# Two low pieces of a weight matrix are made only after the first division by the softmax sums

## The chip, the cores and the metric

The kernel runs on one core of one Trainium2 chip. The metric is the time of one execution in microseconds (us), measured on the device; a kernel's time is the median of several runs. Beside the times there is one execution recorded by the hardware profiler, whose span runs from its first to its last instruction. The core has TensorE (PE, matrix products), VectorE (DVE), ScalarE (ACT), GpSimd (POOL) and SyncE (SP, which here only issues DMA transfers). Each engine runs its instructions in the order written; they wait for each other by semaphores.

## The reference, cut to what matters

The input x has 2048 rows of 640 numbers. Attention with a sliding window of 256 keys (32 heads of 20 numbers) and an MLP with a squared relu follow each other, twice, with the same weights both times:

```python
x = x + A(layernorm(x), wqkv, wo)
x = x + B(layernorm(x), w1, b1, w2, b2)
x = x + A(layernorm(x), wqkv, wo)
x = x + B(layernorm(x), w1, b1, w2, b2)

# A: 32 heads, causal, window of 256
q, k, v = split(x @ wqkv)
p = softmax(where(mask, q @ k.T * 20 ** -0.5, -1e9))
return (p @ v) @ wo
# B: 640 -> 1536 -> 640
h = relu(x @ w1 + b1)
return (h * h) @ w2 + b2
```

The order of the work that the change touches belongs to the start of the first layer: while the first rows go through attention, the weights are still being read and converted.

## The kernel before, in words

**Units and stages.** The rows are cut into 8 groups of 256, and the two layers make 16 units (u = 0 to 15). A unit goes through queries and keys (`stage_qk`), values (`stage_v`), scores, exponentials and products with the values in 8 "quads" of four heads (`max_quad`, `exp_quad`, `pv_quad`), the division by the softmax sums (`load_o`), the output projection with the residual sum and the second layernorm (`stage_o`, `stage_y`), and the MLP (`stage_f`). Units overlap: while the quads of unit u run, TensorE fills its gaps with the dense matrix products of the units beside it (`together`; for the first unit `flow`).

**Halves of 16 bits.** Each float32 matrix is split into a high half, a float16 copy, and a low half, the float16 residual. A product is then three matmuls: high times high, high times low, low times high (`mm3`, L327). For a weight the split is `convert` (L257): ScalarE writes the high half (L259), then VectorE writes the residual (L260).

**The second MLP matrix.** `load_w2` reads w2 in 12 pieces c = 0 to 11, each of 128 x 640 numbers, into five staging places: two in value buffers of later units (pieces 0 and 1) and three in the key buffer of unit 2 (the others, each place several times). The loads are issued on ScalarE's queue (L312). A piece that uses a place again is loaded after the residual of the piece that had it: piece 6 after piece 3, piece 7 after piece 4, then 9 after 6 and 10 after 7. After pieces 7 to 11 the key buffer is filled with a constant (`set_row`, L96, on VectorE), and then the keys of unit 2 are loaded into it (`spread` in `leave`, L548, on SP). After pieces 0 and 1 VectorE fills the sum columns in the two value buffers (L85, L86), which the values of unit 2 need. `stage_f` of unit 0 needs the pieces of w2 one by one.

**The division.** `pv_quad` leaves the products with the values and the sums in device memory. `load_o` reads them back (L871, L872) and divides in four quarters of 64 columns: the reciprocal of the sums (`ratio`, L904, VectorE), the product (`times`, L907, VectorE), the high half (`high`, L911, ScalarE), the low half (`low`, L914, VectorE). The list `js` holds the four low-half jobs. `stage_o` of a unit waits for the first two quarters, makes 30 matmuls with `wo` for the first 128 rows, adds the result to the residual stream (L939), starts a layernorm on it (L353 to L366), and does the same for the other 128 rows. `stage_y` turns the normalised rows over on TensorE (L391), with copies by L377 (ScalarE) and L378 (VectorE).

**The scores.** They are computed twice: once for the row maxima (matmuls L653 into the banks `bb`, maxima L633 on VectorE, eight for each quad), once for the exponentials (matmuls L757 or L765 into the same banks, L779 on ScalarE, masks L794 and L798 on GpSimd). A quad's products with the values are L828, copied out by L840 on ScalarE.

**The planner.** The order of instructions on each engine is fixed when the program is built. The work is posted as jobs with an engine, an estimated cost, the jobs that they depend on and a priority (0 is first, 2 last). `pump` places jobs at the planner's own clock: of the jobs that can start within the next 250 ns, it takes the first by priority; another job of that engine goes ahead of it only if it ends before the first can start. Residuals of w2 have priority 2, the division of unit 0 has priority 1 (its first two high halves 0), the maxima and the layernorms of `stage_o` 1, the additions L939 0. A job may also hold a list `gates` of marks that become done when it does. Three such marks hold loads of weights back already (`gate`, `gate0`, `gate2`):

```python
def put(self):
    t = self.start() + self.cost
    self.fn()
    clk[self.eng] = t
    self.end = t + TAIL[self.eng]
    ...
    for g in self.gates:
        g.end = self.end
```

Of the kernel before, what the change touches and what calls it, by code (L numbers as in the profile page):

```python
# [14 lines left out]
ALU = mybir.AluOpType  # L15
# [3 lines left out]
S = 2048  # L19
D = 640  # L20
# [25 lines left out]
def kernel(ctx: ExitStack, tc: tile.TileContext, x, wqkv, wo, w1, b1, w2, b2, out):  # L46
# [37 lines left out]
    def set_sums(i):  # L84
        nc.vector.memset(vts[i][0][:, :, DH:DH + 1], 1.0 / OS)  # L85
        nc.vector.memset(vts[i][1][:, H * (DH + 1):], 0.0)  # L86
# [8 lines left out]
    def set_row(i, k):  # L95
        nc.vector.memset(krow[i][:, 512 * k:512 * (k + 1)], PAIR)  # L96
# [36 lines left out]
    def post(eng, cost, fn, *deps, wait=0.0, prio=1, **kw):  # L133

        j = Job(eng, cost, fn, [d for d in deps if d is not None], now[0] + wait, prio, **kw)
        k = len(pend)
        while k and pend[k - 1].prio > prio:
            k -= 1
        pend.insert(k, j)
        return j  # L140

    def bulk(fn, size, *deps, **kw):

        return post("A", 400.0, fn, *deps, prio=2, size=size, idle=True, land=WLAND, **kw)

    def dma(fn, size, *deps, n=1, cost=450.0, prio=1, **kw):

        return post("S", n * cost, fn, *deps, prio=prio, size=size, **kw)
# [98 lines left out]
    w2_s = sb.tile([P, 2, FC, D], F16, name="w2_s")  # L247
# [6 lines left out]
    hraw = sb.tile([P, 2 * FC * T // 2], F32, name="stg", tag="hh", bufs=1)  # L254
    gate, gate0, gate2 = [Job("S", 0.0, None, [], 0.0, 0) for i in range(3)]

    def convert(st, hi, low, n, load, *deps, prio=2):  # L257

        a = post("A", 20 + 0.9 * n, lambda: nc.scalar.activation(hi, st, AF.Copy, scale=WS), load, *deps, prio=prio)  # L259
        return post("D", 30 + 1.04 * n, lambda: nc.vector.scalar_tensor_tensor(low, st, WS, hi, op0=ALU.mult,  # L260
                                                                               op1=ALU.subtract), a, prio=prio)

    wqj, woj, w1j, w2j = {}, {}, {}, {}

    def load_wq():
        at = 0
        for lo, n in [(j * D + c, min(2 * P, D - c)) for c in (0, 2 * P, 4 * P) for j in range(2)] + [
                (2 * D + c, min(2 * P, D - c)) for c in (0, 2 * P, 4 * P)]:
            raw, o = (w1raw, at) if at + KC * n <= FC * D else (krow[2], at - FC * D)
            at += KC * n  # L270
            st = raw[:, o:o + KC * n].rearrange("p (c n) -> p c n", c=KC)
            load = dma(lambda st=st, lo=lo, n=n:
                       nc.sync.dma_start(st, wqkv[:, lo:lo + n].rearrange("(c p) n -> p c n", p=P)),
                       P * KC * n * 4, prio=0, land=WLAND)
            for z in range(0, n, P):
                c = slice(lo + z, lo + z + P)
                wqj[(lo + z) // P] = convert(st[:, :, z:z + P], wq_s[:, 0, :, c], wq_s[:, 1, :, c], KC * P, load,
                                             prio=1)
# [3 lines left out]
    def load_wo():  # L282

        v = wo.rearrange("(h c d) n -> d h c n", c=KC, d=4)
        raw = w2raw[:, (FC - KC) * D:].rearrange("p (c n) -> p c n", n=D)
        loads = []
        for d in range(4):
            loads.append(bulk(lambda d=d: nc.scalar.dma_start(raw[d * H:(d + 1) * H], v[d]), H * KC * D * 4, gate0))
        for c in range(KC):
            woj[c] = convert(raw[:, c], wo_s[:, 0, c], wo_s[:, 1, c], D, loads[-1], *loads[:-1])  # L290
        rowset[1] = [post("D", 460, lambda k=k: set_row(1, k), prio=2) for k in range(4)]
# [11 lines left out]
                                 load, *first)  # L303

    sums = []

    def load_w2():
        used_by = {}
        for c, place in enumerate((3, 4, 0, 1, 2, 0, 1, 2, 0, 1, 2, 0)):
            first = [w1j[f] for f in (c // 4 * 2, c // 4 * 2 + 1, 6 + c // 4 * 2, 7 + c // 4 * 2)]  # L310
            st = vts[1 + place][1][:, :D] if place > 2 else krow[2][:, D * place:D * (place + 1)]
            load = bulk(lambda st=st, c=c: nc.scalar.dma_start(st, w2[c * P:(c + 1) * P, :]), P * D * 4,  # L312
                        *([w2j[used_by[place]]] if place in used_by else [gate] if place > 2 else [gate, gate2]))
            w2j[c] = convert(st, w2_s[:, 0, c], w2_s[:, 1, c], D, load, *first)
            used_by[place] = c
        sums.extend(post("D", 130, lambda i=i: set_sums(4 + i), w2j[used_by[3 + i]], prio=2) for i in range(2))

# [85 lines left out]
    def xsrc(l, b):  # L403
        return x_rows[b * P:(b + 1) * P, :] if l == 0 else xs[b]
# [452 lines left out]
    def load_o(u, late=False, free_=()):  # L857

        l, g = divmod(u, NG)
        if late:  # L860
            val = sb.tile([P, KC, T], F32, name="ov", tag="qt", bufs=2)
            od = sb.tile([P, KC, 2, T], F16, name="od", tag="yT", bufs=1)
        else:
            raw = sb.tile([P, 2, KC, T], F32, name="od", tag="hh", bufs=1)
            val = raw[:, 0]
            od = raw[:, 1].rearrange("p c n -> p (c n)").bitcast(F16).rearrange("p (c a n) -> p c a n", a=2, n=T)
        wrote = [ojobs.pop((u, qd)) for qd in range(1, NQ, 2)]
        rs = sb.tile([P, T], F32, name="rs", bufs=1)

        def load():  # L870
            nc.sync.dma_start(rs, ods[u][DH:].to_broadcast([4, H, T]))  # L871
            nc.sync.dma_start(val, ods[u][:DH].rearrange("(c d) h n -> (d h) c n", d=4))  # L872

        loaded = dma(load, P * (KC + 1) * T * 4, *wrote, *free_, n=2, prio=0)
        if u == NU - 1:
            both = sb.tile([P, 2, D], F32, name="x1", tag="qt", bufs=2)
            x1 = [both[:, i] for i in range(2)]
        elif u == NU - 2:

            x1 = [krow[(u - 1) % 3][:, i * D:(i + 1) * D] for i in range(2)]  # L880
        else:
            x1 = [sb.tile([P, D], F32, name="x1", bufs=2) for i in range(2)]
        xj = {}

        def load_x(i, *deps):
            xj[i] = dma(lambda: nc.sync.dma_start(x1[i], xsrc(l, 2 * g + i)), P * D * 4, *deps, prio=2)

        for i in range(2):

            k = 2 * u + i - 2  # L890
            if k < 0 or u >= NU - 2:
                load_x(i, *([loaded] if u == 0 else wrote if u == NU - 1 else ()))
            elif k < len(stored):
                load_x(i, stored[k])
            else:
                waiting[k] = lambda k=k, i=i: load_x(i, stored[k])


        js = []
        for i in range(4):  # L900
            q = slice(i * T // 4, (i + 1) * T // 4)

            def ratio(q=q):
                nc.vector.reciprocal(rs[:, q], rs[:, q])  # L904

            def times(q=q):
                nc.vector.tensor_tensor(val[:, :, q], val[:, :, q],  # L907
                                        rs[:, q].unsqueeze(1).to_broadcast([P, KC, T // 4]), op=ALU.mult)

            def high(q=q):  # L910
                nc.scalar.copy(od[:, :, 0, q], val[:, :, q])  # L911

            def low(q=q):
                nc.vector.tensor_sub(od[:, :, 1, q], val[:, :, q], od[:, :, 0, q])  # L914

            pr = 2 if u else 1
            j = post("D", 575, ratio, loaded, prio=pr)
            j = post("D", 409, times, j, prio=pr)
            j = post("A", 360, high, j, prio=0 if i < 2 else pr)
            js.append(post("D", 402, low, j, prio=pr))  # L920
        ols[u] = od, x1, js, xj
        if u == 0:
            rowset[2] = [post("D", 460, lambda k=k: set_row(2, k), *[w2j[c] for c in (7, 8, 9, 10, 11)], prio=2) for k in range(4)]
            for j, load_ in held:
                load_(loaded, *(rowset[2] if j else ()))
# [273 lines left out]
    load_wo()  # L1199
    load_w1()  # L1200
    load_w2()


# [18 lines left out]
    for n in range(NQ):  # L1222
        todo += [("s", n)] + ([("r", n + LEAD - GQ)] if n % GQ == 1 else []) + [("m", n + LEAD), ("v", n)]
    flow(todo, rest)
    load_o(0)
    dma(lambda: nc.sync.dma_start(b1s, b1.rearrange("(c p) -> p c", p=P)), 8192, *ols[0][2], prio=2)

    while not all(j.end is not None and j.end <= now[0] + LOOK for j in bbjobs):
        c = next(rest)
# [54 lines left out]
```

## Time and profile before

| what | us |
|---|---|
| median of 3 runs | 1586.17 |
| the runs | 1585.07 to 1589.79 |
| the profiled execution | 1588.33 |
| its span | 1586.6 |

| engine | busy us | share of the span |
|---|---|---|
| TensorE, matmuls | 1558.1 | 98% |
| TensorE, weight loads | 1168.7 | 74% |
| VectorE | 984.7 | 62% |
| ScalarE | 734.3 | 46% |
| GpSimd | 600.3 | 38% |

The granted TensorE clock was 0.995 of full speed on average. "Busy" counts instructions from start to end, so overlapping ones on one engine count once; a wait in brackets behind a row is idle time of that engine just before it, and the name behind the arrow is what released it. Names such as L260 are lines of the kernel before. In the page the tiles of the weight `w2` and `w1` carry the name `w_s`, and staging in the key buffers the name `kt`.

### The profile page before, as it was taken

The page shows a single profiled execution, that of the slowest core. Times are in us where ns is not written, and L with a number is a line of the kernel's source. Part 1 is how long each engine was busy: PE and PEld are TensorE (multiplying, and loading weights), DVE is VectorE, ACT ScalarE, POOL GpSimd, SP SyncE. Part 2 cuts the span into 40 slices and gives each one's busy share as a digit, 9 for nine tenths or more (in the row PEclk, how much of TensorE's full clock was granted, in tenths as well). Part 3 has the DMA queues.
Part 4 walks back from the last instruction along what each step waited for, and adds up shares of the span by engine and source line. Part 5 has one row for each costly group of instructions (what it writes and reads, how often), then busy time and mean ns, then how long its engine had stood idle before and what let it go on. Part 6 is the DMA issues. An engine that isn't in the chain of part 4 may idle for free. (4 is left out here: it accounts for less than half of the span.)

```text
span 1586.6 us, 52541 instructions
## 1 busy us (share of the span) xinstructions
PE 1558.1 (98%) x21570; PEld 1168.7 (74%) x21570; DVE 984.7 (62%) x3254; ACT 734.3 (46%) x1593; POOL 600.3 (38%) x1291
## 2 busy tenths in 40 slices
PE   8899999999999999999999999999999999999989
PEld 7666777777777777777777777777778777676767
DVE  8776665666756656565566656657665666756532
ACT  4455545444454444535443453444535345354512
POOL 1233534235253443524324252442525325254512
PEclk9998999999999999999999999999999999999999
DMA  9764343362533525354352534535343343431020
GB/s 272 191 181 117 77 107 86 96 131 55 122 87 103 111 57 127 78 124 90 91 132 64 121 87 110 104 70 128 68 125 83 97 111 69 114 87 58 29 67 18
DMA packets 243353, 160.44 MB, mean 101 GB/s; under 512 B 91176, under 2 KB 226856, under 8 KB 243112
## 3 DMA queue, kind: packets, MB, share of 16 engines
q1 hardware_dynamic: 236744, 147.58, 38.8%
q10 hardware_dynamic: 6368, 9.50, 2.1%
q8 instruction: 169, 2.77, 0.7%
q14 instruction: 72, 0.59, 0.1%
HBM read 84.68 MB, written 52.95 MB: 87 GB/s over the span
## 5 line engine op out<-in xcount | busy, mean ns | idle before, releaser
L779 ACT ACTIVATE pt<-bb 128x512 f32<-128x512 f32 (+1 forms) x736 | 376.0, 600 | 227.0 <-PE bb L757 197.8
L633 DVE CUSTOM_DVE_ANT_0 bb<-bb,maskq 128x320 f32<-128x320 f32 x896 | 409.2, 524 | 86.8 <-PE bb L653 74.6
L794 POOL TENSOR_SCALAR_AFFINE_SELECT pt<-pt 128x256 f32<-128x256 f32 x448 | 188.0, 422 | 563.1 <-ACT pt L779 550.3
L327 PE MATMUL acc<-y,w_s 128*128 128x256 f16 x2880 | 328.3, 273 | 2.5 <-ACT y L377 1.4
L327 PE MATMUL acc<-w_s,hh 128*128 128x320 f16 (+1 forms) x2340 | 326.1, 297 | 0.0
L327 PEld LDWEIGHTS <-w_s 128*128 128x128 f16 x2880 | 276.5, 98 | 54.4 <-issue 18.1
L327 PEld LDWEIGHTS <-hh 128*128 128x128 f16 x2340 | 222.1, 98 | 96.8 <-issue 11.5
L327 PEld LDWEIGHTS <-wq_s 128*128 128x128 f16 x2400 | 229.9, 98 | 46.3 <-issue 13.5
L327 PE MATMUL acc<-yT,wq_s 128*128 128x256 f16 x2250 | 258.6, 273 | 2.2 <-DVE qd L510 0.8
L798 POOL TENSOR_SCALAR_AFFINE_SELECT pt<-pt 128x256 f32<-128x256 f32 x512 | 213.7, 439 | 93.0 <-ACT pt L779 91.6
L1013 DVE TENSOR_TENSOR hh<-r,hh 128x256 f16<-128x256 f32 x192 | 95.1, 517 | 208.8 <-ACT hh L1010 201.8
L828 PE MATMUL pv<-pt,vt 128*32 128x128 f32 (+1 forms) x3840 | 190.9, 331 | 1.2 <-POOL pt L798 1.2
L1007 POOL TENSOR_TENSOR r<-r 128x256 f32<-128x256 f32 x192 | 114.2, 615 | 161.2 <-ACT r L1003 158.8
L840 ACT COPY ot<-pv 128x256 f32<-128x256 f32 x128 | 47.7, 373 | 268.8 <-PE pv L828 268.7
L327 PE MATMUL acc<-wo_s,od 128*128 128x320 f16 x960 | 141.7, 303 | 4.8 <-ACT od L911 3.0
L633 DVE DVE_READ_ACCUMULATOR2_ANT mx<- 128x1 f32 x1024 | 145.1, 142 | 0.0
L828 PEld LDWEIGHTS pv<-pt,vt 128*32 128x32 f32 x3840 | 105.4, 110 | 41.7 <-POOL pt L798 6.5
L327 PE MATMUL acc<-wq_s,yT 128*128 128x320 f16 x900 | 132.0, 299 | 1.4 <-DVE y L378 0.9
L327 PEld LDWEIGHTS <-od 128*128 128x128 f16 x960 | 92.1, 99 | 51.0 <-issue 6.4
L1003 ACT ACTIVATE r<-acc,b1s 128x256 f32<-128x256 f32 x192 | 80.7, 472 | 87.7 <-PE acc L327 86.4
L327 PEld LDWEIGHTS <-yT 128*128 128x128 f16 x900 | 85.7, 98 | 39.3 <-issue 6.7
L364 POOL TENSOR_TENSOR bmv<-bmv,neghalf 128x1 f32<-128x1 f32 x64 | 45.5, 717 | 136.1 <-DVE bmv L358 135.7
(95 smaller groups left out, 1226.3 us busy)
## 6 DMA issues: line engine op xcount, KB each, us to landing
qt<-qk SPq DMA_DIRECT2D x30, 480.0 KB
kt<-qk SPq DMA_DIRECT2D x30, 480.0 KB
qk<-qd SPq DMA_DIRECT2D x17, 640.0 KB
o<-ot SPq DMA_DIRECT2D x256, 42.0 KB
od<-o SPq DMA_DIRECT2D x14, 640.0 KB
qk<-yl SPq DMA_DIRECT2D x13, 640.0 KB
qk<-qd SPq DMA_DIRECT2D x17, 320.0 KB
xt<-in_A_x_dram SPq DMA_DIRECT2D x16, 320.0 KB
```

Of the source, the lines that this page charges most:

```text
L327: nc.tensor.matmul(acc, lhs(a, c), rhs(b, c), start=(k == 0), stop=(k == 3 * nk - 1))
L364: j = post("G", 520, lambda: nc.gpsimd.tensor_tensor(box["mv"][:, 3:4], box["mv"][:, 2:3], neghalf, op=ALU.pow), j, prio=prio)
L633: nc.vector.tensor_tensor_reduce(out=v, in0=v, in1=mask, scale=1.0, scalar=-3.0e38, op0=ALU.add, op1=ALU.max, accum_out=accum[e, w]),
L779: nc.scalar.activation(box["pt"][:, :o], bb[e][:, k, :o], AF.Exp, scale=SCALE / (QS * QS))
L794: nc.gpsimd.affine_select(out=m, in_=m, pattern=[[0, 2], [-1, P]], compare_op=ALU.is_gt, fill=0.0, base=0, channel_multiplier=1)
L798: nc.gpsimd.affine_select(out=m, in_=m, pattern=[[0, 2], [1, P]], compare_op=ALU.is_ge, fill=0.0, base=0, channel_multiplier=-1)
L828: nc.tensor.matmul(pv[32 * jj:32 * (jj + 1), q0 * P:(q0 + qn) * P], vf[:, c:c + 32], pj[:, j, :], start=(k == 0), stop=(k == len(steps) - ...
L840: nc.scalar.copy(ot[:, qd % 2], pv)
L1003: nc.scalar.activation(box["r"], acc[:, f, :], AF.Relu, bias=b1s[:, f0 + f:f0 + f + 1], scale=1.0 / (YS * WS))
L1007: nc.gpsimd.tensor_tensor(box["r"], box["r"], box["r"], op=ALU.mult)
L1013: nc.vector.tensor_sub(hh[:, 1, f, :], box["r"], hh[:, 0, f, :])
```

## The change

`convert` gets a list `behind`, and its VectorE job, the residual, depends on what is in it as well as on the high half. `load_w2` passes the new mark `divided` for pieces 3 and 4. `load_o` for unit 0 hangs that mark on `js[1]`, the low half of the second quarter. So the residuals of pieces 3 and 4 are placed on VectorE only after the planner has placed that job. Their loads and high halves are as they were, no instruction is added or taken away, and the residuals of all other weights keep their dependencies.

```diff
-    def convert(st, hi, low, n, load, *deps, prio=2):
+    def convert(st, hi, low, n, load, *deps, prio=2, behind=()):
 
         a = post("A", 20 + 0.9 * n, lambda: nc.scalar.activation(hi, st, AF.Copy, scale=WS), load, *deps, prio=prio)
         return post("D", 30 + 1.04 * n, lambda: nc.vector.scalar_tensor_tensor(low, st, WS, hi, op0=ALU.mult,
-                                                                               op1=ALU.subtract), a, prio=prio)
+                                                                               op1=ALU.subtract), a, *behind, prio=prio)
...
     sums = []
+    divided = Job("S", 0.0, None, [], 0.0, 0)
...
-            w2j[c] = convert(st, w2_s[:, 0, c], w2_s[:, 1, c], D, load, *first)
+            w2j[c] = convert(st, w2_s[:, 0, c], w2_s[:, 1, c], D, load, *first, behind=[divided] if c in (3, 4) else [])
...
+        if u == 0:
+            js[1].gates.append(divided)
         ols[u] = od, x1, js, xj
```

## The prediction

> **What bounds the kernel now.** I read the windows first, because the change touches one place early in a long kernel and I need to know how much time any place has to give. The columns are the stretch, its length, then the busy time of TensorE (PE), its weight loads, VectorE (DVE), ScalarE (ACT) and GpSimd (POOL), the granted TensorE clock, the DMA share and GB/s.
>
> ```profile
> 300.00:1500.00 1200.00, 1196.24 (x17161) 898.67 (x17159) 746.26 (x2497) 560.44 (x1222) 475.65 (x1035) 1.00 0.41 95
> 1500.00:1586.60 86.60, 79.28 (x753) 61.57 (x750) 25.53 (x57) 23.81 (x56) 21.59 (x40) 1.00 0.13 40
> 113.80:117.20 3.40, 1.35 (x46) 0.95 (x49) 2.82 (x9) 2.26 (x5) 3.40 (x6) 1.00 0.71 226
> 117.20:127.60 10.40, 8.12 (x54) 4.32 (x44) 8.58 (x28) 2.04 (x5) 0.78 (x3) 0.51 1.12 236
> 131.00:137.00 6.00, 6.00 (x89) 4.26 (x91) 4.32 (x12) 3.87 (x8) 4.14 (x9) 1.00 0.01 1
> 144.60:148.00 3.40, 2.68 (x22) 1.74 (x25) 2.14 (x3) 2.02 (x5) 2.15 (x5) 1.00 0.46 141
> 171.00:177.30 6.30, 6.30 (x102) 4.92 (x95) 5.42 (x21) 3.27 (x8) 2.38 (x6) 1.00 0.81 153
> ```
>
> From 300 to 1500 us TensorE is idle for 1200 - 1196.24 = 3.8 us and at the end for 7.3 us: it is the bound, and a VectorE edit can gain only where TensorE still waits. The one bad place is 113.8 to 127.6: first a stretch with TensorE 1.35 of 3.40 us busy, then 10.4 us at half the clock. The division of unit 0 lies in it, so I read each engine in order of time there, TensorE first. Columns: start, duration, engine, line, operation, tiles, shapes, count, and in brackets the idle time before it with what ended it.
>
> ```profile
> 116.79 2.45 PE L828 MATMUL pv<-pt,vt 128*32 128x256 f32 x32
> 121.52 7.23 PE L327 MATMUL acc<-wo_s,od 128*128 128x320 f16 x30 [2.27 <-ACT od L911]
> ...
> 129.47 4.24 PE L327 MATMUL acc<-wo_s,od 128*128 128x320 f16 x30
> ```
>
> The first 30 matmuls of the output projection waited 2.27 us for the second high piece of the divided values, and took 7.23 us where the next 30 took 4.24 us. Wait and slow clock are worth 2.27 + 2.99 = 5.3 us: all that could be won here. The question is whether the two residuals stand in the way. VectorE, then ScalarE:
>
> ```profile
> 113.22 1.76 DVE L260 SCALAR_TENSOR_TENSOR w_s<-kt,w_s 128x640 f16<-128x640 f32 x2
> 114.90 0.41 DVE L510 SCALAR_TENSOR_TENSOR qd<-acc,qd 128x256 f16<-128x256 f32 x1
> ...
> 117.02 0.50 DVE L633 CUSTOM_DVE_ANT_0 bb<-bb,maskq 128x320 f32<-128x320 f32 x1 [0.58 <-PE bb L653]
> ...
> 117.44 0.55 DVE L904 RECIPROCAL rs<-rs 128x64 f32<-128x64 f32 x1
> ```
>
> ```profile
> 119.31 0.37 ACT L840 COPY ot<-pv 128x256 f32<-128x256 f32 x1 [3.25 <-PE pv L828]
> 119.58 0.46 ACT L911 CAST od<-od 128x320 f16<-128x320 f32 x1
> ...
> 123.02 1.39 ACTq L312 DMA_DIRECT2D kt<-in_B_w_dram  x3
> ```
>
> Pieces 2 and 3 of the second MLP matrix are the two at 113.22, piece 4 comes right behind the L510. None of them delays the division: behind them VectorE is idle for 0.58 us, waiting for TensorE's scores (L653), and takes the first maximum and then the first reciprocal at 117.44. ScalarE's first cast L911 stands behind its copy L840, which waited for the end of the 32 matmuls that began at 116.79. So the chain to 121.52 runs TensorE, copy, cast, not through the residuals.
>
> **The change, step by step.** All durations are from the profiled execution, whose time is 1588.33 us, 2.2 us over the median of 1586.17 us; the sum is a difference, which I add to the median.
>
> *The two residuals leave the place before the division.* VectorE is free 0.8 us (half of the 1.76 us) earlier for the L510 at 114.90 and again for the sums' fills. What follows waits for TensorE anyway (the 0.58 us above becomes 0.58 + 1.64 = 2.2 us, with 0.82 us for a piece from the rows below), so the gain is 0. It can't be a loss; as a gain it is bounded by the 2.27 us that TensorE waits.
>
> *The order around them.* The planner gives a place to the first job in order of priority that starts within its 250 ns of looking ahead, and puts a lower one before it only if it ends in time. By its own times the maximum at 117.02 fits ahead of the reciprocal with or without the residuals. So I expect the same order on all engines up to the second low piece of the division, which opens the gate. From there the two jobs have the lowest priority (2), so the rest of the division, eight maxima and the projection's additions go first:
>
> ```profile
> 131.71 0.49 DVE L939 SCALAR_TENSOR_TENSOR x<-acc,x 128x320 f32<-128x320 f32 x1 [0.22 <-PE acc L327]
> 132.48 0.68 DVE L366 TENSOR_SCALAR xt<-x,bmv 128x640 f32<-128x640 f32 x1 [0.28 <-POOL bmv L364]
> 133.75 0.49 DVE L939 SCALAR_TENSOR_TENSOR x<-acc,x 128x320 f32<-128x320 f32 x1 [0.59 <-PE acc L327]
> ...
> 135.39 0.82 DVE L260 SCALAR_TENSOR_TENSOR w_s<-kt,w_s 128x640 f16<-128x640 f32 x1
> 136.67 0.61 DVE L366 TENSOR_SCALAR xt<-x,bmv 128x640 f32<-128x640 f32 x1 [0.45 <-POOL bmv L364]
> ...
> 140.74 0.83 DVE L260 SCALAR_TENSOR_TENSOR w_s<-kt,w_s 128x640 f16<-128x640 f32 x1
> 141.48 0.89 DVE L378 TENSOR_TENSOR y<-tr,y 128x384 f16<-128x384 f32 x2
> ```
>
> The row at 135.39 shows where a job of that priority lands: among the layernorms. Counting the planner's costs on (30 + 1.04 x 640 = 696 ns for a residual), I put the two between the third and the fourth addition, one on each side of the L366 at 132.48. They take 2 x 0.82 = 1.64 us and find 0.28 + 0.59 us of idle there: 1.64 - 0.87 = 0.77 us is left. The fourth addition, its statistics, the L366 at 136.67 and the eight maxima end that much later. Who waits:
>
> ```profile
> 140.91 0.78 PE L757 MATMUL bb<-qt,kt 62*64 62x192 f16 x32
> 142.09 2.20 PE L327 MATMUL acc<-wq_s,yT 128*128 128x320 f16 x15 [0.40 <-DVE y L378]
> ...
> 145.77 2.20 PE L327 MATMUL acc<-wq_s,yT 128*128 128x320 f16 x15 [0.52 <-DVE y L378]
> ```
>
> The L757 overwrites the banks that the maxima read, and it starts just when they end, so TensorE waits up to 0.77 us more, and the exponentials behind it pass the delay on to 145.77. Cover for the pieces was 0.87 us of idle; with none it costs all 1.64 us; below, if the next piece's residual (140.74) drops out of the way of the L378 and both TensorE waits vanish, the step gains 0.40 + 0.52 = 0.92 us. I take +0.77, the count by rows.
>
> *Loads behind the residuals.* Pieces 6 and 7 reuse the staging of 3 and 4. Their loads are two of the three issues at 123.02, in the stretch with a DMA share of 1.12; now they stand on ScalarE's queue behind the residuals, from about 133 us, where the share is 0.01. ScalarE must hold at each issue until the residual is done. It gains nothing, since TensorE has no wait between 129.47 and 137. It costs nothing as long as the holds lie in ScalarE's own waits; bound above 1.64 us, both residuals in full, below 0.
>
> *The chain to the third unit's keys.* Pieces 6 to 11 follow, then the fills of the staging with the constant (L96), then the load of unit 2's keys over it (L548), then their first scores:
>
> ```profile
> 159.96 1.36 ACT L259 ACTIVATE w_s<-kt 128x640 f16<-128x640 f32 x2
> ```
>
> ```profile
> 167.65 2.10 DVE L96 MEMSET kt<- 128x512 f32 x4 [0.17 <-DVE w_s L260]
> ```
>
> ```profile
> 169.78 0.91 SPq L548 DMA_DIRECT2D kt<-qk x2
> ```
>
> ```profile
> 169.75 1.00 PE L653 MATMUL bb<-kt,qt 60*64 60x256 f16 x38
> ...
> 179.91 0.76 PE L653 MATMUL bb<-kt,qt 60*64 60x256 f16 x38
> ```
>
> The key traffic ends near 177.3 (the window above, share 0.81), 2.6 us ahead of the L653. The high halves of the last two pieces run only at 159.96, some 27 us behind the new place of the loads of pieces 6 and 7, so a slip of a few us of the loads is taken up. Cost 0; above it, see the third rival.
>
> *The sum.* 0 + 0.77 + 0 + 0 = +0.8 us: 1586.17 + 0.77 = 1586.9 us. A difference of 0.3% is 4.8 us, about what a measurement of this kernel can tell from no change (its three runs lie 4.7 us apart); the forecast is no change. From the unknown terms its own range is 1586.17 - 0.92 = 1585.2 to 1586.17 + 1.64 + 1.64 = 1589.5; later order adds about 2 us on both sides, 1583 to 1592.
>
> **The rivals.**
>
> *The stall goes.* If ScalarE's first cast or the first reciprocal does get ahead, the wait of 2.27 us and the slow clock go: 1586.17 - 5.3 = 1580.9 us. For it: the change points at this place, and VectorE is busy from 113.22 on. Against it: the 0.58 us of idle behind the residuals and the 3.25 us wait of L840. It decides if TensorE's wait at 121.52 falls below 1 us.
>
> *A second slow spell.* TensorE was slowed after a stretch with 1.35 of 3.40 us busy (40%). The stretch 144.6 to 148.0 has 2.68 us, and 1.91 us (56%) with 0.77 us more wait. If that is too little, another spell costs the 2.99 us seen above: 1586.9 + 3.0 = 1589.9 us, with the doubled wait of the bounds 1591.5. Against it: 56% is more than 40%, and 2.68 us kept the clock at 1.00. [...]
>
> *The keys come late* (the slower side). If a residual of pieces 8 to 11 misses its place before a group of eight maxima, it goes behind the next group; TensorE's score groups L653 are about 10 us apart here (169.75 and 179.91). A slip of 10 us less the 2.6 us of slack makes the L653 wait 7.4 us: 1586.9 + 7.4 = 1594.3 us. For it: four more jobs of lowest priority are pushed on. Against it: the planner knows the keys' load and fills in other matmuls first. It decides once the keys' load is issued later than 172.4 us (169.78 + 2.6).
>
> *A later order that differs.* From 131.7 us on the planner's clock differs by some tenths, and 14 units follow whose pieces may be interleaved otherwise. TensorE's idle of 3.8 and 7.3 us bounds a gain at 11 us; a loss has no such bound. To pass 4.8 us either way would need about half of that idle, or as much again.
>
> **How the numbers follow.** No change as summed 0.48; the stall goes 0.16; second spell 0.10; late keys 0.16; another later order beyond 0.3%: 0.05 faster, 0.05 slower. Faster is 0.16 + 0.05 = 0.21. The second spell lies on the border of 1590.9 and I count it as slower: 0.10 + 0.16 + 0.05 = 0.31. The range runs from just below the first rival, 1580.5, to just above the third, 1595.0; outside are the far parts of the last case and of the rivals, some 0.15.
>
> **What would show it.** Right: VectorE's wait before the maximum at 117.02 grows to about 2.2 us and the reciprocal still starts at 117.4; TensorE's wait of 2.27 us and the spell of half clock stay; the two L260 stand near 132 to 134.5, and the L757 at 140.91 starts 0.3 to 0.8 us later; two L312 issues move from 124 to 133 us or later; the first L653 on unit 2's keys waits for no DMA. Wrong: a reciprocal before 117, a granted clock other than 0.51 in 117 to 128 or below 1 after 141, keys issued after 172.4, or more than 7.3 us of TensorE idle at the end.

## The result and the profile after

| | before | after |
|---|---|---|
| median us | 1587.82 (22 runs) | 1590.53 (22 runs) |
| the runs | 1584.34 to 1592.43 | 1587.09 to 1593.61 |
| the profiled execution | 1588.33 | 1591.18 |
| its span | 1586.6 | 1589.4 |

The ratio is 1.0016 with a 95% interval of 1.0009 to 1.0024: some 2.5 us slower (0.0016 x 1587.8), between 1.4 and 3.8. That is a real loss, and smaller than the 0.3% at which the prediction drew its line. Lines of the changed kernel are shifted: L260 is still L260, but L653 is L654, L757 is L758, L911 is L912, L939 is L942. The kernels of the experiments keep the numbers of the kernel before.

From 300 us to the end nothing points at the change. In the windows view of the changed kernel TensorE is idle for 1200 - 1194.47 = 5.5 us in the long stretch (3.8 us before), but in a second profile of the changed kernel, which comes below, it is 3.8 us again, and the order of all instructions behind some 200 us is the same in both kernels. The loss is near the place of the change:

```profile
109.23:112.64 3.41, 1.25 (x43) 0.92 (x46) 1.05 (x6) 2.41 (x6) 3.28 (x8) 1.00 0.76 167
112.64:122.88 10.24, 7.94 (x52) 4.12 (x45) 8.16 (x26) 2.05 (x5) 0.00 (x0) 0.50 1.13 266
...
136.54:139.95 3.41, 2.02 (x40) 1.36 (x38) 3.41 (x13) 1.61 (x4) 0.00 (x0) 1.00 0.35 98
139.95:143.36 3.41, 3.41 (x14) 1.96 (x13) 0.16 (x1) 2.12 (x5) 2.65 (x7) 0.50 0.07 25
...
300.00:1500.00 1200.00, 1194.47 (x17140) 897.32 (x17139) 747.66 (x2499) 559.31 (x1220) 475.24 (x1034) 1.00 0.41 95
```

The stretch of 10.24 us at half clock is still there, behind a stretch with TensorE 1.25 of 3.41 us busy. A second one of 3.41 us has come up at 139.95, behind a stretch with 2.02 us busy.

To measure a place inside a long kernel I take the time between two landmarks that both kernels have: the first scores of the exponentials of unit 1 (the group at L765, L766 after) and those of its sixth quad (L757, L758 after). TensorE's order of time, first before, then after:

```profile
111.65 0.83 PE L765 MATMUL bb<-qt,kt 62*128 62x256 f16 x16
...
175.21 0.75 PE L757 MATMUL bb<-qt,kt 62*64 62x192 f16 x32
```

```profile
107.30 0.83 PE L766 MATMUL bb<-qt,kt 62*128 62x256 f16 x16
...
117.39 7.02 PE L328 MATMUL acc<-wo_s,od 128*128 128x320 f16 x30 [2.30 <-ACT od L912]
124.97 2.74 PE L328 MATMUL acc<-wo_s,od 128*128 128x320 f16 x19 [0.56 <-DVE x L942]
127.64 0.75 PE L758 MATMUL bb<-qt,kt 62*64 62x192 f16 x32
...
128.43 1.66 PE L328 MATMUL acc<-wo_s,od 128*128 128x320 f16 x11
...
138.24 0.24 PE L758 MATMUL bb<-qt,kt 62*64 62x192 f16 x1 [0.59 <-DVE mx L634]
138.68 0.75 PE L758 MATMUL bb<-qt,kt 62*64 62x192 f16 x31 [0.21 <-DVE mx L634]
139.83 3.87 PE L328 MATMUL acc<-wq_s,yT 128*128 128x320 f16 x15 [0.40 <-DVE y L379]
...
145.19 2.20 PE L328 MATMUL acc<-wq_s,yT 128*128 128x320 f16 x15 [0.52 <-DVE y L379]
...
175.04 0.75 PE L758 MATMUL bb<-qt,kt 62*64 62x192 f16 x32
...
179.74 0.76 PE L654 MATMUL bb<-kt,qt 60*64 60x256 f16 x38
```

Before, the way takes 175.21 - 111.65 = 63.56 us; after, 175.04 - 107.30 = 67.74 us. (That the changed kernel reached the first landmark 4.35 us earlier has nothing to do with the change: the two orders are the same up to there, and the other profiles reach it between 107.3 and 111.6 us.) Three things are new in these rows:

- The order. Before, 30 matmuls of the output projection, 32 scores, 30 more. Now 49, then the 32 scores, then 11. Behind the 30th TensorE waits 0.56 us for the first addition to the residual stream (L942).
- The third group of scores waits 0.59 + 0.21 = 0.80 us for the row maxima.
- The 15 matmuls at 139.83 take 3.87 us instead of 2.20: the second stretch of half clock, 1.67 us.

Together they make 3.03 of the 4.18 us by which the way has grown; the other 1.15 us is spread over the rest of the way and not assigned to a cause.

VectorE's order of time shows where the order comes from:

```profile
112.67 0.50 DVE L634 CUSTOM_DVE_ANT_0 bb<-bb,maskq 128x320 f32<-128x320 f32 x1 [2.38 <-PE bb L654]
...
113.09 0.55 DVE L905 RECIPROCAL rs<-rs 128x64 f32<-128x64 f32 x1
...
124.42 0.89 DVE L942 SCALAR_TENSOR_TENSOR x<-acc,x 128x320 f32<-128x320 f32 x2 [2.49 <-PE acc L328]
125.23 0.49 DVE L634 CUSTOM_DVE_ANT_0 bb<-bb,maskq 128x320 f32<-128x320 f32 x1
...
126.43 0.81 DVE L260 SCALAR_TENSOR_TENSOR w_s<-kt,w_s 128x640 f16<-128x640 f32 x1
127.20 0.49 DVE L942 SCALAR_TENSOR_TENSOR x<-acc,x 128x320 f32<-128x320 f32 x1
...
129.67 0.80 DVE L260 SCALAR_TENSOR_TENSOR w_s<-kt,w_s 128x640 f16<-128x640 f32 x1
...
132.18 1.05 DVE L260 SCALAR_TENSOR_TENSOR w_s<-kt,w_s 128x640 f16<-128x640 f32 x1
134.41 0.62 DVE L367 TENSOR_SCALAR xt<-x,bmv 128x640 f32<-128x640 f32 x1 [1.18 <-POOL bmv L365]
```

The first two additions stand at 124.42, ahead of the eighth maximum at 125.23; before, all eight maxima came ahead of them. Whatever stands behind the eighth maximum, the scores of the next quad above all, was planned later by that, and the planner put 19 more projection matmuls in front. ScalarE's queue changed too: the load of piece 5 is now issued between the third and the fourth cast of the division, and those of pieces 6 and 7 come behind the two residuals:

```profile
116.88 0.86 ACT L912 CAST od<-od 128x320 f16<-128x320 f32 x2 [0.98 <-DVE od L908]
117.29 0.34 ACTq L313 DMA_DIRECT2D kt<-in_B_w_dram  x1
118.88 0.46 ACT L912 CAST od<-od 128x320 f16<-128x320 f32 x1 [1.15 <-DVE od L908]
127.31 0.34 ACTq L313 DMA_DIRECT2D kt<-in_B_w_dram  x1
...
130.51 0.34 ACTq L313 DMA_DIRECT2D kt<-in_B_w_dram  x1
```

### The profile page after: what moved, and what is told of

Read it like the earlier page. It is cut to its first block, busy times and chain, and to the rows that moved or that the text cites. A ratio compares the mean times of both kernels' runs of the same rounds, so it can differ in the third digit from the quotient of the medians.

```text
span 1589.4 us, 52543 instructions
## 1 busy us (share of the span) xinstructions
PE 1559.3 (98%) x21570; PEld 1169.7 (74%) x21570; DVE 985.7 (62%) x3254; ACT 734.2 (46%) x1593; POOL 600.2 (38%) x1291
## 5 line engine op out<-in xcount | busy, mean ns | idle before, releaser
L634 DVE DVE_READ_ACCUMULATOR2_ANT mx<- 128x1 f32 x1024 | 141.8, 138 | 0.0
```

Of the source, the lines that this page charges most:

```text
L634: nc.vector.tensor_tensor_reduce(out=v, in0=v, in1=mask, scale=1.0, scalar=-3.0e38, op0=ALU.add, op1=ALU.max, accum_out=accum[e, w]),
```

## The experiments

Theory A: the loss is the order that the planner chose (first addition ahead of the eighth maximum, scores behind 19 more matmuls). Theory B: the late residuals, and the loads behind them, cost time themselves. Theory C, a form of A: in the new order the 31st projection matmul needs the bank that the first addition frees, and that addition needs rows of the residual stream whose load lands late; the load of piece 5, now in front, makes it later. Of the edits that several kernels share, each diff shows only what is new. "Ratio" is to the kernel before.

**The order alone.** The planner sees the changed kernel, and the instructions of residuals 3 and 4 are written right behind that of piece 2, where they stood.

```diff
+        write = lambda: nc.vector.scalar_tensor_tensor(low, st, WS, hi, op0=ALU.mult, op1=ALU.subtract)
+        return post("D", 30 + 1.04 * n, place(write) if place else write, a, *behind, prio=prio)
...
+            w2j[c] = convert(..., place={2: lambda f: lambda: [g() for g in [f, *early]],
+                                         3: lambda f: early.append(f) or (lambda: None),
+                                         4: lambda f: early.append(f) or (lambda: None)}.get(c))
```

> The whole order of the changed kernel on TensorE, ScalarE and GpSimd, but the two residuals are written where the kernel before has them, right behind that of piece 2. Theory A (the loss comes from the order that the planner chose around the residuals: the first addition ahead of the eighth maximum, the scores of the next quad behind 19 more matmuls): as slow as the changed kernel, ratio to before 1.0010 to 1.0020, and the wait of the 31st output projection matmul for the addition (0.56 us in the changed kernel) is there. Theory B (the loss comes from the residuals themselves, late on VectorE among the layernorms): ratio 0.9995 to 1.0005, the maxima of quad 12 end as early as before and no second spell of half clock follows.

1592.04 us against 1587.97, ratio 1.0024 [1.0014, 1.0035]. The whole loss is there with the residuals in their old place. TensorE, then VectorE:

```profile
130.47 2.74 PE L327 MATMUL acc<-wo_s,od 128*128 128x320 f16 x19 [1.95 <-DVE x L939]
```

```profile
129.92 0.89 DVE L939 SCALAR_TENSOR_TENSOR x<-acc,x 128x320 f32<-128x320 f32 x2 [3.24 <-DMA x<-in_A_x_dram]
```

Here the addition waits for its load by name, and TensorE waits 1.95 us for the addition. (In the profile of the changed kernel the wait before 124.42 is put down to TensorE; but the first addition needs only the first 15 of the 30 matmuls, so there too it may have been the load.)

**The move alone.** The planner sees the kernel before; the jobs of residuals 3 and 4 only put their instructions into the list `early`, and these are written behind the second low half of the division.

```diff
-                nc.vector.tensor_sub(od[:, :, 1, q], val[:, :, q], od[:, :, 0, q])
+                nc.vector.tensor_sub(od[:, :, 1, q], val[:, :, q], od[:, :, 0, q]); [f() for f in early if u == 0 and q.start == T // 4]
```

> The order of the kernel before on TensorE, ScalarE and GpSimd, and the two residuals written directly behind the second low piece of the division. Theory A: ratio 0.9995 to 1.0005. Theory B: residuals in this place delay the maxima but not the layernorms; also 0.9995 to 1.0005, with the eight maxima 1.5 us later and TensorE's second group of 30 matmuls on time. A third view, that the division itself gains once the residuals are gone from ahead of it: ratio below 0.998 and TensorE's wait of 2.27 us gone.

1587.74 us, ratio 0.9999 [0.9987, 1.0012]. The division doesn't start sooner for VectorE's free time: TensorE still waits 2.62 us for the cast (2.27 before).

**The changed kernel with the addition held behind the maxima** in the plan; the residuals stay late.

```diff
-    lambda wait: jobs.append(post("D", 408, add, xj[i], wait=wait, prio=0)))
+    lambda wait: jobs.append(post("D", 408, add, xj[i], *(bbjobs if u + i + h == 0 else ()), wait=wait, prio=0)))
```

> The changed kernel, and in the plan the first addition of the first output projection comes behind the eighth maximum, which gives TensorE the order of the kernel before (30, scores, 30) while the residuals stay late among the layernorms and the loads of pieces 6 and 7 stay behind them. Theory A: ratio 0.9995 to 1.0005. Theory B: 1.0008 to 1.0020, with TensorE waiting 0.5 to 0.8 us for the maxima of quad 12.

1587.47 us, ratio 0.9996 [0.9984, 1.0007]. The order is 30 (2 and 28), 32 scores, 30 again and the loss is gone, though residuals and loads 6 and 7 are late:

```profile
118.27 0.45 PE L327 MATMUL acc<-wo_s,od 128*128 128x320 f16 x2 [2.27 <-ACT od L911]
118.99 3.98 PE L327 MATMUL acc<-wo_s,od 128*128 128x320 f16 x28 [0.28 <-DVE od L914]
122.90 1.16 PE L757 MATMUL bb<-qt,kt 62*64 62x192 f16 x32
...
124.22 4.23 PE L327 MATMUL acc<-wo_s,od 128*128 128x320 f16 x30
```

With the two experiments above this falls to A and against B.

**The kernel before with the new order.** The planner counts the load of the first unit's residual stream at half its size; the load itself is as it was.

```diff
-    xj[i] = dma(lambda: nc.sync.dma_start(x1[i], xsrc(l, 2 * g + i)), P * D * 4, *deps, prio=2)
+    xj[i] = dma(lambda: nc.sync.dma_start(x1[i], xsrc(l, 2 * g + i)), P * D * 4 // (2 if u == 0 else 1), *deps, prio=2)
```

> The kernel before, with its residuals in their place, and in the plan alone the loads of the residual stream for unit 0 count half their size, so that the planner puts the first addition ahead of the eighth maximum; TensorE gets the order of the changed kernel (49 matmuls, scores, 11). Theory A: ratio 1.0008 to 1.0020 and a wait of about 0.5 us for the addition. Theory B: 0.9995 to 1.0005.

1588.62 us, ratio 1.0008 [0.9999, 1.0016]. This one edit of a planned time gives the order 49, scores, 11, so a load that is planned some tenths earlier is enough to turn it. The loss is about half, with an interval that takes in no loss; TensorE waits only 0.18 us for the addition. The order by itself is not the whole price.

**Load 5 behind the fourth cast again**, the rest as changed.

```diff
-    sums = []
+    sums = []; cast4 = Job("S", 0.0, None, [], 0.0, 0)
...
-                        *([w2j[used_by[place]]] if place in used_by else [gate] if place > 2 else [gate, gate2]))
+                        *([w2j[used_by[place]]] if place in used_by else [gate] if place > 2 else [gate, gate2]), *([cast4] if c == 5 else ()))
...
-            j = post("A", 360, high, j, prio=0 if i < 2 else pr)
+            j = post("A", 360, high, j, prio=0 if i < 2 else pr); j.gates += [cast4] if u + 3 - i == 0 else []
```

> The changed kernel with one difference: on ScalarE the load of piece 5 stands behind the fourth high half of the division again, not behind the third, so that it no longer goes out between the two loads of the residual stream. Theory C (the loss is the wait of the 31st projection matmul for an addition whose operand is late, and the operand is late because the load of piece 5 gets ahead of it): ratio to before at most 1.0008, as with the early addition alone, and the wait for the addition is below 0.3 us. If the position of that load does not matter: 1.0013 to 1.0024, and the wait stays at 0.5 to 2 us.

1589.57 us, ratio 1.0012 [1.0003, 1.0021]. The wait for the addition isn't in its profile; the 0.80 us wait for the maxima and the second stretch of half clock are. The place of load 5 is at most a part. (That the wait is missing here says little: the second profile of the changed kernel, below, lacks it with load 5 in front.)

**The residual stream's load first.** In the changed kernel it is issued ahead of the query load of unit 2 on SP.

```diff
-    xj[i] = dma(lambda: nc.sync.dma_start(x1[i], xsrc(l, 2 * g + i)), P * D * 4, *deps, prio=2)
+    xj[i] = dma(lambda: nc.sync.dma_start(x1[i], xsrc(l, 2 * g + i)), P * D * 4, *deps, prio=2 if u else 0)
```

> The changed kernel, with the two loads of the residual stream for unit 0 issued ahead of the query load of unit 2 on SP (priority 0 instead of 2), which takes the wait for the operand away at its source. Theory A in the form of C: the first additions start right behind TensorE's products, TensorE's wait for the addition is gone (0 to 0.1 us), ratio 0.9990 to 1.0006. If the loss sits in the scores that come 19 matmuls later, whatever the operand does: 1.0010 to 1.0020.

1588.08 us, ratio 1.0002 [0.9992, 1.0011]. SP, TensorE, VectorE:

```profile
112.49 2.38 SPq L886 DMA_DIRECT2D x<-in_A_x_dram  x2
```

```profile
118.31 8.23 PE L327 MATMUL acc<-wo_s,od 128*128 128x320 f16 x47 [0.27 <-DVE od L914]
```

```profile
121.23 0.49 DVE L939 SCALAR_TENSOR_TENSOR x<-acc,x 128x320 f32<-128x320 f32 x1 [0.91 <-PE acc L327]
```

The load is issued 112.49 - 108.57 = 3.9 us behind the first landmark of this kernel (8.1 in the changed one, at 115.37), the addition waits for its matmuls alone, and the 47 matmuls run through without a wait. The order is still 49, scores, 11. So, by the medians, this order is dear only as long as the residual stream is late: A, in the form of C. The profiles alone wouldn't show it: the second one of the changed kernel, below, has no wait for the addition either, and its way is 64.84 - 63.47 = 1.37 us longer, no more than one slow window.

**Filling the stall.** 23 matmuls of the next unit go into the gap ahead of the division.

```diff
-    parts += [some(rest, left_over - 9e3), stage_o(0), ...
+    parts += [some(rest, left_over - 5e3), stage_o(0), ...
```

> The changed kernel with more of the values of unit 2 placed ahead of the first output projection (5 us held back instead of 9). The sums' columns are filled earlier since the residuals left, so 23 matmuls go into TensorE's first gap before the maxima's scores and 7 into the wait for the division. All theories of the loss leave it open; from the wait of 2.3 us and the spell at half clock (5.3 us by the prediction) a gain of 2 to 6 us, ratio 0.996 to 0.999, and no granted clock of 0.5 in that place.

1607.04 us, ratio 1.0126 [1.0110, 1.0142]: a miss, some 20 us. The stall at the division is shorter, but TensorE meets the next one at once, and then a far dearer one. TensorE, then SP:

```profile
117.26 4.50 PE L327 MATMUL acc<-wo_s,od 128*128 128x320 f16 x30 [0.53 <-ACT od L911]
126.34 2.29 PE L327 MATMUL acc<-wo_s,od 128*128 128x320 f16 x8 [4.58 <-DVE x L939]
...
198.62 0.65 PE L653 MATMUL bb<-kt,qt 60*64 60x128 f16 x33 [1.08 <-DMA kt<-qk]
```

```profile
191.16 1.12 SPq L548 DMA_DIRECT2D kt<-qk  x2
```

The keys of unit 2 are loaded at 191.16 instead of 169.78, since the pieces of w2 that use the same buffer came late, and all 144 matmuls of the MLP's second product went ahead of the next scores, where it had been 16. TensorE's wait for the keys themselves is only 1.08 us; what is dear is that nothing is left to fill the waits behind it, and TensorE is busy for 72.96 of the 85 us from 165 us on (84.36 in the kernel before). The late keys are the prediction's third rival, in a kernel that brought it about; that they cost the 20 us is read from these rows and was not tried by itself.

**The first copy behind the first cast** on ScalarE, with the addition held. The list `casts` holds the high halves of the division.

```diff
-        jobs.append(post("A", 262, out, prio=0))
+        jobs.append(post("A", 262, out, *(casts[:1] if n == NQ else ()), prio=0))
```

> The changed kernel with the first addition pinned behind the maxima, and ScalarE's copy of the first quad of unit 1 placed behind the first high half of the division. By the prediction's reading of the chain (products with the values, copy, cast) the cast no longer waits for TensorE: the wait of 2.3 us falls to 1.0 to 1.5 us, ratio 0.9985 to 0.9997. If the division waits for its data instead, the wait stays at 2.2 us or more and the ratio is 0.9995 to 1.0005.

1588.04 us, ratio 1.0004 [0.9995, 1.0013]. TensorE's wait for the cast falls from 2.27 to 1.66 us, between the two forecasts (1.0 to 1.5 us, or 2.2 us and more), and the time doesn't move by what can be measured. The copy was only part of the chain: now the cast waits 2.49 us for the product on VectorE, whose reciprocal stands behind the first maximum, and that one waited 2.38 us for TensorE's scores. No run puts the reciprocal ahead of that maximum.

**Only piece 4's residual behind the division.**

```diff
-    behind=[divided] if c in (3, 4) else []
+    behind=[divided] if c == 4 else []
```

> Only piece 4's residual is ordered behind the division; piece 3's stays where it was. TensorE's order is then that of the kernel before (30 projection matmuls, 32 scores, 30), although the piece 4 residual and the loads behind it are late. Theory A (the loss is TensorE's order): ratio 1.000 (0.999 to 1.001), no wait of TensorE for the addition of the residual stream. Theory B (the late residuals and loads themselves cost): about half of the loss, 1.0008, with a wait of the score matmuls of the fifth quad for the maxima.

1587.54 us, ratio 1.0001 [0.9990, 1.0012]. The order is 30, scores, 30, no wait for additions or maxima. It fits A; a B of half the loss lies within the interval, so this run alone wouldn't decide. It also shows which of the two residuals turns the order: piece 3's, which stands ahead of the L510, and here stays there.

**The changed kernel a second time**, for another profile.

> The changed kernel once more (the same instructions in the same order), for a second profile and more runs. If the loss is TensorE's order alone: 1.0016 again (1.0009 to 1.0024), steps of about 20, 10.5 and 14 us from the first to the fourth exponential group, a wait for the first addition. Whether the second stretch of half clock near 140 us comes again: if it is part of the loss it is there and the step from the third to the fourth group is 14.5 us; if it is chance, that step is 12.5 us and the ratio the same.

1590.00 us, ratio 1.0017 [1.0008, 1.0027]: the loss comes again. But its profile differs. TensorE, then a window:

```profile
108.69 0.83 PE L765 MATMUL bb<-qt,kt 62*128 62x256 f16 x16
...
119.64 8.23 PE L327 MATMUL acc<-wo_s,od 128*128 128x320 f16 x47 [0.27 <-DVE od L914]
...
138.41 0.24 PE L757 MATMUL bb<-qt,kt 62*64 62x192 f16 x1 [0.59 <-DVE mx L633]
138.85 0.75 PE L757 MATMUL bb<-qt,kt 62*64 62x192 f16 x31 [0.21 <-DVE mx L633]
140.00 2.20 PE L327 MATMUL acc<-wq_s,yT 128*128 128x320 f16 x15 [0.40 <-DVE y L378]
...
173.53 0.75 PE L757 MATMUL bb<-qt,kt 62*64 62x192 f16 x32
```

```profile
137.73:141.14 3.41, 2.21 (x42) 1.66 (x42) 2.55 (x9) 1.83 (x5) 0.71 (x2) 1.00 0.27 96
```

The way between the landmarks takes 173.53 - 108.69 = 64.84 us, 1.28 more than before and 2.90 less than in the first profile. The 0.80 us for the maxima is the same; the wait for the addition and the second stretch of half clock are not there. They come in some of the profiled executions only.

**Two tries for a faster kernel:** the load early, and 15 matmuls of the next unit ahead of the projection; first in the changed kernel with the addition held, then in the kernel before.

```diff
+    xj[i] = dma(..., prio=2 if u else 0)
-    parts += [some(rest, left_over - 9e3), stage_o(0), ...
+    parts += [some(rest, left_over - 7e3), stage_o(0), ...
```

> The changed kernel with the additions held behind the maxima in the plan, the loads of the residual stream ahead of unit 2's query load, and 15 matmuls of the next unit put into the gap ahead of the division instead of behind it. Theory A says: the 4.58 us wait for the addition seen with the fill alone was its late operand, so it goes, while the first slow stretch stays away; TensorE then has 2 to 5 us less idle and slow time, minus what the 15 matmuls are missing later (in the order from 170 us on nothing differs): ratio 0.997 to 1.000. The rival (the place gives nothing since each gap filled here opens another a few matmuls on): 1.000 to 1.003.

> The kernel before with the loads of the residual stream early and 15 matmuls of the next unit ahead of the projection, but behind the products of the first quad; the residuals stand where they stood. If the stall at the division can be bought off without touching the residuals: 0.997 to 0.999, the first projection matmul waits under 1 us, clock in 117 to 128 over 0.8. If the half clock comes anyway, since it follows the gap ahead of the scores and not the wait for the cast: 0.999 to 1.002 with a clock near 0.5 there.

1604.03 us, ratio 1.0100 [1.0081, 1.0119], and 1599.90 us, ratio 1.0081 [1.0067, 1.0096]: both missed. Windows of the second, then of the kernel before:

```profile
113.00:128.00 15.00, 14.29 (x142) 9.08 (x135) 11.96 (x38) 5.43 (x13) 2.80 (x8) 0.92 0.95 219
...
165.00:250.00 85.00, 72.06 (x999) 51.12 (x994) 48.49 (x158) 31.46 (x66) 25.35 (x56) 0.92 0.39 89
```

```profile
113.00:128.00 15.00, 10.56 (x103) 6.04 (x101) 12.44 (x38) 5.04 (x12) 4.75 (x8) 0.66 1.01 234
...
165.00:250.00 85.00, 84.36 (x1269) 62.30 (x1259) 56.14 (x183) 40.72 (x87) 33.57 (x76) 1.00 0.43 102
```

In the second kernel the stall at the division is bought off (14.29 of 15 us busy at a clock of 0.92 against 10.56 at 0.66). In the first it isn't: the 15 matmuls went ahead of the maxima's scores, TensorE still waits 2.74 us for the cast, and the two windows from 116.76 on run at 0.50. In both more is lost behind 165 us; in the second the keys' load comes at 183.95 and TensorE is busy for 72.06 of 85 us. As in the kernel that fills the stall, nearly all the matmuls of the MLP's second product (140 of 144, and all 144) then go ahead of the scores that need the keys. No kernel here is measurably faster than the kernel before.

All profiles with the landmark way, by order of the projection; "slow" counts stretches of 3.41 us at half clock, between 110 and 128 us and between 135 and 146 us:

| kernel | order | way us | wait for addition | wait for maxima | slow | ratio |
|---|---|---|---|---|---|---|
| before | 30, 30 | 63.56 | 0 | 0 | 3, 0 | 1 |
| move alone | 30, 30 | 63.75 | 0 | 0 | 3, 0 | 0.9999 |
| addition held | 30, 30 | 62.17 | 0 | 0.17 | 1, 0 | 0.9996 |
| copy behind cast | 30, 30 | 62.68 | 0 | 0.17 | 2, 0 | 1.0004 |
| only piece 4 | 30, 30 | 63.40 | 0 | 0 | 2, 0 | 1.0001 |
| changed | 49, 11 | 67.74 | 0.56 | 0.80 | 3, 1 | 1.0016 |
| changed, again | 49, 11 | 64.84 | 0 | 0.80 | 2, 0 | 1.0017 |
| order alone | 49, 11 | 66.53 | 1.95 | 0.21 | 2, 0 | 1.0024 |
| load 5 behind | 49, 11 | 66.66 | 0 | 0.80 | 2, 1 | 1.0012 |
| before, new order | 49, 11 | 64.04 | 0.18 | 0.21 | 2, 0 | 1.0008 |
| stream's load first | 49, 11 | 63.47 | 0 | 0.72 | 1, 0 | 1.0002 |

The five with the old order take 63.1 us on the mean, the six with the new one 65.5 us: 2.4 us. Their ratios differ by 0.0013 on the mean, 2.1 us. (In the last row 0.51 us of the wait stands under a DMA's name, and so does the 0.17 us of "copy behind cast"; the maxima on VectorE end just then.)

## Why the prediction was right or wrong

No change beyond 0.3% was forecast and came, and the range holds 1590.53 us (1580.5 to 1595.0). The size was not: +0.77 us was forecast, 2.5 us (1.4 to 3.8) came, and the range of the likeliest case, 1585.2 to 1589.5, didn't hold it. Of the 3.6 us between 1586.9 and 1590.53, 1.65 us is the base: the kernel before has a median of 1587.82 us over 22 runs, not the 1586.17 us of the three shown. As a difference, 2.5 us lies within the sum's own bounds, -0.92 to +3.28 us.

*The residuals leave the place before the division: 0.* Right. VectorE's wait ahead of the maximum grew from 0.58 to 2.38 us (2.2 forecast). The reciprocal stands 113.09 - 107.30 = 5.79 us behind the first landmark, and stood 117.44 - 111.65 = 5.79 us behind it before. TensorE's wait for the cast is 2.30 us, and the clock behind it 0.50.

*The order around them.* This is the step that failed, at the sentence "I expect the same order on all engines up to the second low piece", and at the one that puts the maxima ahead of the additions. I asked which VectorE jobs the freed time would let pass, and looked at maximum and reciprocal only. The L510 between the residuals leads to the query write, then the query load, then the residual stream's load, all on SP. The planner counts the bytes of these transfers one behind the other, so an earlier query write makes it expect the residual stream earlier, and then the addition (priority 0) is ready ahead of the eighth maximum (priority 1). That the order follows that load's planned time is shown by the kernel that counts the load at half its size. That the freed L510 is what moved it is shown by "only piece 4": piece 3's residual still stands ahead of the L510, which comes 112.06 - 108.82 = 3.24 us behind the first landmark (3.25 before, 2.48 in the changed kernel), and the order is the old one. The planner's own times, which the kernels work out when they are built, agree: the residual stream is expected at 115.15 us before and with only piece 4 moved, and at 114.61 us in the changed kernel, and the eighth maximum's place is at 115.00 us. On the chip the load was later in one profile and earlier in the other: it was issued 7.33 us behind the first landmark before, and 8.07 and 6.59 us behind it in the two profiles of the changed kernel.

*The 0.77 us at the L757.* It measured 0.59 + 0.21 = 0.80 us, in both profiles of the changed kernel, but not by the sum as I made it. The residuals stand at 126.43 and 129.67, the first ahead of the third addition and the second ahead of the fourth, and piece 5's follows at 132.18. In the old order late residuals cost 0 to 0.17 us there, and in the new order residuals in their old place cost 0.21. It takes both. That 0.80 us came where 0.77 was forecast is luck: the two residuals landed elsewhere, and the old order would have cost 0.17 us at most.

*Loads behind the residuals: 0.* Those of pieces 6 and 7 moved from 123.02 to 127.31 and 130.51, and no wait of TensorE names them. Counted from the first landmark, which this profile reaches 4.35 us earlier, that is 131.7 and 134.9 in the times of the kernel before (133 or later forecast). That the load of piece 5 would go in front of the fourth cast was missing.

*The chain to the third unit's keys: 0.* Right: the L653 on them (L654, at 179.74) waits for nothing. SP issues the load just ahead of the same scores as before:

```profile
169.59 0.91 SPq L549 DMA_DIRECT2D kt<-qk  x2
```

Counted from the first landmark it is 62.29 us, 4.2 us more than before and so past the sign of 172.4, but TensorE's own way is 4.18 us longer and the slack is kept. The prediction gave its signs in the times of one profile; they have to be counted from a landmark.

*The rivals.* The stall did not go. The second slow spell, at 0.10, came in one of two profiles of the changed kernel, at 1.67 us instead of 2.99, and one stretch earlier than foreseen: it lies on the matmuls right behind the scores that wait for the maxima, not behind the second wait for L378 (145.77 before). In that profile the granted clock changes at 112.64, 122.88, 139.95 and 143.36, so 10.24, 17.07 and 3.41 us apart: 3, 5 and 1 times 3.41. Between 136.54 and 139.95, ahead of the second fall, no gap of TensorE is longer than 0.59 us. Cut into windows of 3.41 us along these edges, the two profiles differ: with the same wait of 0.80 us, the window before 139.95 holds 2.02 us of work in the first, and in the second the work is cut at 137.73 and no window from 127.49 to 144.55 falls below 2.21. That the work in one window decides is a reading of these two and was not tried. The keys came late in none of the two profiles, but in the three kernels that fill the stall: the load at 191.16 in one of them, past the 172.4 at which I said it decides, and the kernels were 12.6 to 19.8 us slower.

What stays open: how the 2.5 us divides on the mean between the waits for the addition and for the maxima and the slow windows. Two profiles show two different sums (4.18 and 1.28 us more than the one of before), and the unprofiled runs show none. By the medians the wait for the late load should be the larger part, since the kernel with the stream's load first keeps 0.72 us of wait for the maxima and loses nothing that can be measured; yet the two profiles have it at 0.56 and 0. The slow windows can't be much of it on the mean. Every run gives its mean granted clock: 0.9966 over the 34 runs of the changed kernel, 0.9967 over the 83 runs of the kernel before beside the experiments. One more window at half clock would lower that mean by about 0.0011 (half of 3.41 of 1587 us), so with the spread of these runs the changed kernel has half a window more at most.

## What to carry to other kernels

Where a planner writes the order, moving one instruction off an engine moves the planned times of all that follows it, on other queues too. Follow each of those chains to the first place where two jobs of unlike priority could change places, loads of operands included, before saying that the order stays. And where TensorE has run out of independent work, the three tries here to fill the place with matmuls from a later one gave nothing back: look first at who needed them there, and at what else the planner moves.

## What was not expected of the hardware

In the changed kernel the clock halved behind 3.41 us in which TensorE's longest wait was 1.94 us (109.23 to 112.64), and behind 3.41 us in which it was 0.59 us (136.54 to 139.95). In all fourteen profiles each stretch at half clock between 100 and 149.5 us is one, two or three times 3.41 us long, and where a profile has several, they start multiples of 3.41 us apart (6.8 to 27.3 us). Against the program this raster lies otherwise in each profile: the first slow window begins 4.25 to 5.78 us behind the first landmark in ten of the eleven profiles of the table, and 10.58 us behind it in the other. After the windows at full clock quoted with 1.25 and 2.02 us of work the clock halved, after the one with 2.21 it did not. Inside the changed kernel's 10.24 us at half clock the first two windows hold 2.45 and 2.08 us, and the clock stayed at 0.50. Busy time alone isn't the measure, though. The kernel with the addition held has this window, at full clock, with the next one at full clock too:

```profile
116.75:120.16 3.41, 1.61 (x11) 0.98 (x12) 3.33 (x10) 1.30 (x4) 0.00 (x0) 1.00 1.19 204
120.16:123.57 3.41, 3.27 (x38) 2.15 (x40) 3.39 (x15) 0.07 (x1) 0.00 (x0) 1.00 1.10 263
```

Its 1.61 us are projection matmuls on 128 x 128 tiles; the 2.02 us in the changed kernel are 0.99 us of scores on 62 x 64 tiles, 0.91 us of float32 transposes and a rest. That the kind of work makes the difference fits these two windows and was not tried; behind 1.47 us of projection matmuls (117.25 to 120.67 in the changed kernel's second profile) the clock was 0.50. So a wait of 0.80 us costs 0.80 us in one profile and 0.80 + 1.67 in another. The stall at the division has one, two or three slow windows (table). That this is one of the reasons why the runs of the kernel before lie 8 us apart fits their mean clocks: of the 83 runs, the 13 with 0.995 or less have a median of 1590.0 us, the 24 with 0.998 or more one of 1586.9.

Between two profiles with the same order, the start of the kernel up to the first landmark differs by up to 4.35 us, more than the whole effect under study. Only the way between landmarks around the change, over several profiles, could be held against the medians.
